# Folding the key weights in two half-height array tiles, and the last chunk's last products by column halves

## The chip, the cores and the metric

The kernel runs on one core of a Trainium2 chip. Its time is the device time of one execution, in microseconds (us). The matrix engine is called PE (its weight loads PEld), the vector engine DVE, the scalar engine ACT, GpSimd POOL, and SP is the engine whose queue issues most transfers. PE writes its results to PSUM, which is cut into banks of 128 partitions by 512 floats; ACT and DVE read them from there.

## The reference

For x of 2048 rows and 512 columns the reference returns `g * a + (1 - g) * b`, with a gate `g = sigmoid(sum(x * gate_w))` for each row.

`a` is linear attention with 32 heads of 16 columns:

```python
pk = einsum("bhsd,hdf->bhsf", k, w_phi)          # the same for q
phi_k = concatenate([softmax(pk), softmax(-pk)])
kv = einsum("bhsf,bhsd->bhfd", phi_k, v);  z = phi_k summed over s
o = (phi_q @ kv) / (phi_q @ z + 1e-6);  a = o @ wo
```

`b` is a feed-forward layer of width 1792: `relu(x @ w1 + b1) ** 2 @ w2 + b2`.

`pk` is `x @ wk` and then a 16 by 16 matrix for each head, so the two weights can be multiplied once, ahead of all rows: `x @ (wk w_phi)`. That product is the fold.

## The kernel before

**Precision.** Each float operand is split into a rounded high part and the rest (`split`, L58: ACT copies the high part, DVE subtracts it for the low part). A product is three matmuls (`mm3`, L66 to L70): high with high, high with low, low with high.

**Stages.** The feed-forward width is worked in two sweeps of 7 pieces of 128; each sweep passes over four row blocks of 512 rows. `work_list` (L510) lists these 56 steps. A step has an "up" product (`up`, 4 x 3 matmuls into bank `u`), relu and square on ACT and a split (`hidden`, L301), and two steps later a "down" product (`down`, L316) into four banks `d0` to `d3`, one for each chunk of 128 rows. The attention work is dealt between these steps: `at(slot, f)` (L464) puts a function at a half step. In the first sweep come the key fold, and for each chunk of 128 rows the key projection (`do_k`), its exponentials (`exps`, L191), the value projection (`do_v`) and the sum over rows (`do_kv`); in the second come the queries.

**The fold.** `load_fold` brings the transposed weight in four row tiles and `w_phi` as a block-diagonal matrix. `fold` (L138) makes the folded weight for one piece k of 128 rows: four float matmuls of 128 rows by 128 columns into one bank, then one split of 512 columns into `wkh`, `wkl`. `do_fold` (L323) is called for k = 0, 1 at slot 3 and for k = 2, 3 at slot 4 (L473), so that PE sees two blocks of eight matmuls, each put right after an up product. The banks come from two pools, `ps_a` and `ps_b`, in turn (`bank`, L50); after the last key fold `ps_b` is given to the sum over rows, and one bank is left for the key and value projections.

**What sets the order.** The framework orders the work of each engine by priority and by dependences that it finds; `tc.high_priority` lifts the splits, and `tc.issue_after` puts work behind a named instruction. Each engine works its own list in order. Tiles of a pool are reused in turn, so that a transfer into a buffer waits until the last reader of the buffer's previous content is done: the four `in` buffers are freed by the low-part subtractions on DVE.

**The end.** In the last step the products of the last two pieces are done chunk by chunk (L540 to L543), six matmuls of 512 columns for each. After each chunk DVE scales and adds the result (L560). For the last chunk that is done in two column halves, each with its own transfer to the output, one issued by SP and one by ACT.

A float matmul (not one of the rounded type) appears as two records in the profile: the 32 key-fold records are 16 matmuls.

Of the kernel before, what the change touches and what calls it, by code (L numbers as in the profile page):

```python
# [9 lines left out]
F32R = mybir.dt.float32r  # L10
# [6 lines left out]
P = 128  # L17
S, D, H, DH, F = 2048, 512, 32, 16, 1792
NK = D // P
SB = 512  # L20
NB = S // SB
NC = SB // P
NF = F // P
NFH = NF // 2
# [3 lines left out]
AHEAD = 150  # L28
# [3 lines left out]
def tile_gated_mix(ctx: ExitStack, tc: tile.TileContext, xT, xn, wqT, wkT, wphi, wv, wo, w1, b1, w2, b2, gw, out):  # L32
    nc = tc.nc
# [4 lines left out]
    wpool = pool("wpool", 1)  # L38
# [8 lines left out]
    banks = [ps_a, ps_b]  # L47
    taken = [0]

    def bank(name):  # L50
        p = banks[taken[0] % len(banks)]
        taken[0] += 1
        return p.tile([P, 512], F32, tag="s", name=name)
# [4 lines left out]
    def split(src, hi, lo, ehi, elo):  # L58
        if ehi is nc.scalar:
            i = nc.scalar.activation(hi, src, AF.Copy)  # L60
        else:
            i = ehi.tensor_copy(hi, src)
        elo.tensor_tensor(lo, src, hi.bitcast(F32), ALU.subtract)  # L63
        return i

    def mm3(o, a, b, sa, sb, first, last):  # L66
        (ah, al), (bh, bl) = a, b
        nc.tensor.matmul(o, ah[:, sa], bh[:, sb], start=first, stop=False)  # L68
        nc.tensor.matmul(o, ah[:, sa], bl[:, sb], start=False, stop=False)  # L69
        return nc.tensor.matmul(o, al[:, sa], bh[:, sb], start=False, stop=last)  # L70

    ALL = slice(0, 512)
    halves = (slice(0, 256), slice(256, 512))
# [7 lines left out]
    def row():  # L81
        return work.tile([P, D], F32, tag="row", name="row", bufs=6)
# [26 lines left out]
    st, up_w, down_w = {}, {}, {}  # L109
# [28 lines left out]
    def fold(loaded, nm, k):  # L138
        wph, *t = loaded
        ps = bank(f"fold{nm}{k}")  # L140
        for g in range(NK):
            nc.tensor.matmul(ps[:, g * P:(g + 1) * P], t[g][:, k * P:(k + 1) * P], wph[:, g * P:(g + 1) * P],
                             start=True, stop=True)
        hi = wpool.tile([P, 512], F32R, tag=f"wah{k}", name=f"w{nm}h{k}")
        lo = wpool.tile([P, 512], F32R, tag=f"wal{k}", name=f"w{nm}l{k}")
        with tc.high_priority(offset=AHEAD):
            split(ps, hi, lo, nc.scalar, nc.vector)
        return hi, lo

    def load_w(src, nm):  # L150
        res = []
        for k in range(NK):
            if nm == "o":

                t = stage.tile([P, 512], F32, tag="in", name="in")
                for q in range(4):
                    s = 64 * (4 * (k % 2) + q) + 32 * (k // 2)
                    nc.sync.dma_start(t[32 * q:32 * q + 32, :], src[s:s + 32, :])
            else:
                t = load(src[k * P:(k + 1) * P, :])  # L160
            hi = wpool.tile([P, 512], F32R, tag=f"wbh{k}", name=f"w{nm}h{k}")
            lo = wpool.tile([P, 512], F32R, tag=f"wbl{k}", name=f"w{nm}l{k}")
            split(t, hi, lo, nc.scalar, nc.vector)
            res.append((hi, lo))
        return res
# [18 lines left out]
    def project(c, xs, ws, nm):  # L184
        ps = bank(nm)
        sc = slice(c * P, (c + 1) * P)
        for k in range(NK):
            mm3(ps, xs[k], ws[k], sc, ALL, k == 0, k == NK - 1)
        return ps
# [99 lines left out]
    def attended(o, u, wos):  # L289
        ps = bank("att")  # L290
        for r in range(2):
            for t in range(2):
                mm3(ps, o[r], wos[2 * r + t], slice((2 * t + u) * P, (2 * t + u + 1) * P), ALL,
                    r + t == 0, r + t == 2)
        return ps


    def up_step(ps, k, xs, wf):
        st["up"] = mm3(ps, wf, xs[k], slice(k * P, (k + 1) * P), ALL, k == 0, k == NK - 1)
# [13 lines left out]
            up_step(ps, k, xs, wf)  # L313
        return hidden(fc, ps)

    def down(t, c, dps):  # L316
        sw, b, i = work_list[t]
        mm3(dps[c], hid[t], down_w[sw * NFH + i], slice(c * P, (c + 1) * P), ALL, i == 0, i == NFH - 1)

    def do_wT(wT):  # L320
        st["wT"] = load_fold(wT)
# [1 line left out]
    def do_fold(nm, k):  # L323
        with tc.issue_after(st["up"].ins):
            st["wa", nm, k] = fold(st["wT"], nm, k)
        if k == NK - 1:
            st["wa"] = [st["wa", nm, i] for i in range(NK)]
            if nm == "k":
                banks.pop()

    def do_w(src, nm):
        st["wb"] = load_w(src, nm)
# [131 lines left out]
    def at(slot, f, *a):  # L464
        steps.setdefault(int(slot), []).append(lambda: f(*a))
# [4 lines left out]
        at(2 * (fc - LAG) - 2, do_w1_first, fc)  # L470
        at(2 * (fc - LAG) - (2 if fc == LAG + 1 else 1), do_w2, fc)
    at(0, do_wT, wkT)
    for k in range(NK):  # L473
        at(3 + k // 2, do_fold, "k", k)
    at(1, do_w, wv, "v")
    for b in range(NB):
        for c in range(NC):
            s = b * SL + 3 * c - 3 if b else 7 + c
# [3 lines left out]
        for c in range(NC):  # L482
            n = b * NC + c
            s = 5 + 2.9 * n
# [5 lines left out]
    for k in range(NK):  # L490
        at(49 + k, do_fold, "q", k)
# [7 lines left out]
    for p in range(NB * NC // 2):  # L499
        n, s = 2 * p, 54 + 6 * p  # L500
# [10 lines left out]
    hid, last = {}, len(work_list) - 1  # L511

    def do_up(t):
        if t < len(work_list):
            sw, b, i = work_list[t]
            fc = sw * NFH + i
            hid[t] = up(fc, st["x", sw * NB + b], up_w[fc])
# [12 lines left out]
    dps = None  # L530
    for t, (sw, b, i) in enumerate(work_list):
        for f in steps.get(2 * t, ()):
            f()
        do_up(t + LAG)
        for f in steps.get(2 * t + 1, ()):
            f()
        if i == 0:
            dps = [ps_d.tile([P, 512], F32, tag="d", name=f"d{c}") for c in range(NC)]

        now = () if t == last - 1 else (t - 1, t) if t == last else (t,)  # L540
        for c in range(NC):
            for u in now:
                down(u, c, dps)  # L543
        if i < NFH - 1:
            continue
        for c in range(NC):
            n = b * NC + c
            done = ("f", n) in st
            if sw == 0:
                o = row()  # L550
                nc.scalar.activation(o, b2b, AF.Copy, scale=rest[:, n:n + 1])
            else:
                if not done:
                    st["f", n] = row()
                    nc.sync.dma_start(st["f", n], part[n])
                o = st["f", n]
            dst = part[n] if sw == 0 else out[n * P:(n + 1) * P, :]
            for j, s in enumerate(halves if n == NB * NC - 1 and done else (ALL,)):
                with tc.high_priority(offset=AHEAD):
                    nc.vector.scalar_tensor_tensor(o[:, s], dps[c][:, s], rest[:, n:n + 1], o[:, s], ALU.mult, ALU.add)  # L560
                if sw == 0 or done:
                    (nc.scalar if j else nc.sync).dma_start(dst[:, s], o[:, s])
# [47 lines left out]
```

## Time and profile before

| what | value |
|---|---|
| median of three timings | 533.31 us (532.88 to 533.75) |
| the profiled execution's own time | 533.63 us |
| its span, first to last instruction | 531.8 us |
| PE busy | 521.5 us, 98% |
| PEld, DVE, ACT, POOL busy | 417.5, 355.9, 234.7, 76.8 us |
| key-fold records on PE (L142) | 32, mean 281 ns |
| granted PE clock | 1.000 |

A row of the timeline has the start in us, the length in us, engine, line, operation, what is written from what, the shape, and how many instructions are merged; square brackets hold the idle time before it and what ended it. PE's matmuls overlap and their ends are modelled, so starts are what to compare: where the engine streams, the next start comes sooner than the length. A row of the waits reads: who waited for whom, total us, times, longest. Groups by line give busy us and mean ns of one, and then the idle time before them. Transfers by issue have KB and the median us from issue to landing.

### The profile page before, as it was taken

The page shows a single profiled execution, that of the slowest core. Times are in us where ns is not written, and L with a number is a line of the kernel's source. Part 1 is how long each engine was busy: PE and PEld are TensorE (multiplying, and loading weights), DVE is VectorE, ACT ScalarE, POOL GpSimd, SP SyncE. Part 2 cuts the span into 40 slices and gives each one's busy share as a digit, 9 for nine tenths or more (in the row PEclk, how much of TensorE's full clock was granted, in tenths as well). Part 3 has the DMA queues.
Part 4 walks back from the last instruction along what each step waited for, and adds up shares of the span by engine and source line. Part 5 has one row for each costly group of instructions (what it writes and reads, how often), then busy time and mean ns, then how long its engine had stood idle before and what let it go on. Part 6 is the DMA issues. An engine that isn't in the chain of part 4 may idle for free.

```text
span 531.8 us, 8944 instructions
## 1 busy us (share of the span) xinstructions
PE 521.5 (98%) x3475; PEld 417.5 (79%) x3475; DVE 355.9 (67%) x608; ACT 234.7 (44%) x404; POOL 76.8 (14%) x60
## 2 busy tenths in 40 slices
PE   8998999999999999999999999999999999999997
PEld 3886888888888887887878878787887878787775
DVE  4688536743465434567579998998878887779423
ACT  3874333622435224254654564353435353535230
POOL 2001111111110011011103121202111111112000
PEclk9999999999999999999999999999999999999999
DMA  7974004200042000415346113134102311023102
GB/s 236 297 240 138 2 0 160 76 6 1 1 159 70 10 1 21 160 41 160 88 139 222 35 41 122 53 118 137 40 22 79 119 51 30 22 70 100 49 1 79
DMA packets 30834, 45.16 MB, mean 85 GB/s; under 512 B 5704, under 2 KB 12360, under 8 KB 30792
## 3 DMA queue, kind: packets, MB, share of 16 engines
q1 hardware_dynamic: 30328, 44.20, 27.0%
q8 instruction: 27, 0.44, 0.3%
q10 hardware_dynamic: 432, 0.39, 0.2%
q14 instruction: 15, 0.12, 0.1%
q0 software_dynamic: 32, 0.01, 0.0%
HBM read 29.89 MB, written 8.39 MB: 72 GB/s over the span
## 4 chain that ended last, share of the span: by engine, by line
PE 72%; DVE 10%; DMA 6%; SPq 5%; ACT 3%; POOL 2%; issue 2%; DVEq 0%; ACTq 0%; POOLq 0%
PE u L68 7%; PE d L69 7%; PE d L70 7%; PE d L68 7%; PE u L70 7%; PE u L69 7%; SPq L257 4%; PE v L68 3%; PE k L68 3%; PE v L69 3%; PE v L70 3%; PE k L70 3%; PE k L69 3%; PE kvps L221 2%; DMA in<-in_xT 2%; PE att L68 2%
## 5 line engine op out<-in xcount | busy, mean ns | idle before, releaser
L303 ACT ACTIVATE r<-u,b1c 128x512 f32<-128x512 f32 x56 | 38.5, 687 | 151.3 <-PE u L70 148.0
L68 PE MATMUL d<-w2h,hh 128*128 128x512 f32 x224 | 87.5, 391 | 0.0
L69 PE MATMUL d<-w2l,hh 128*128 128x512 f32 x224 | 87.3, 390 | 0.0
L70 PE MATMUL d<-w2h,hl 128*128 128x512 f32 x224 | 87.1, 389 | 0.0
L68 PE MATMUL u<-xh,w1h 128*128 128x512 f32 x220 | 86.8, 395 | 0.1
L70 PE MATMUL u<-xh,w1l 128*128 128x512 f32 x220 | 85.7, 390 | 0.5 <-DVE w1l L63 0.5
L69 PE MATMUL u<-xl,w1h 128*128 128x512 f32 x220 | 85.8, 390 | 0.0
L63 DVE TENSOR_TENSOR hl<-r,hh 128x512 fp32r<-128x512 f32 x56 | 43.0, 769 | 54.8 <-ACT hh L60 54.7
L231 POOL TENSOR_TENSOR ez<-e,z 128x512 f32<-128x512 f32 x32 | 41.4, 1317 | 188.3 <-ACT e L204 188.3
L213 POOL TENSOR_TENSOR e<-e,r 128x1024 f32<-128x1024 f32 x16 | 32.3, 2017 | 205.0 <-DVE r L209 158.3
L207 DVE TENSOR_REDUCE sm<-e 128x64 f32<-128x1024 f32 x32 | 39.0, 1218 | 28.5 <-ACT e L204 28.4
L68 PEld LDWEIGHTS u<-xh,w1h 128*128 128x128 f32 x220 | 41.3, 188 | 12.0 <-issue 1.6
L70 PEld LDWEIGHTS d<-w2h,hl 128*128 128x128 f32 x224 | 42.0, 188 | 8.7
L68 PEld LDWEIGHTS d<-w2h,hh 128*128 128x128 f32 x224 | 42.0, 188 | 8.7
L69 PEld LDWEIGHTS d<-w2l,hh 128*128 128x128 f32 x224 | 42.1, 188 | 8.6
L70 PEld LDWEIGHTS u<-xh,w1l 128*128 128x128 f32 x220 | 41.3, 188 | 9.5 <-DVE w1l L63 0.9
L69 PEld LDWEIGHTS u<-xl,w1h 128*128 128x128 f32 x220 | 41.3, 188 | 8.2
L204 ACT ACTIVATE e<-e 128x1024 f32<-128x1024 f32 x32 | 33.8, 1055 | 23.7 <-DVE e L202 23.5
L255 ACT ACTIVATE phiT<-tb 32x256 f32<-32x256 f32 x64 | 26.5, 413 | 35.1 <-DVE tb L249 34.4
L60 ACT ACTIVATE hh<-r 128x512 fp32r<-128x512 f32 x56 | 35.2, 628 | 1.3
L304 ACT ACTIVATE r<-r 128x512 f32<-128x512 f32 x56 | 35.1, 627 | 1.0
L199 DVE TENSOR_REDUCE mx<-k 128x32 f32<-128x512 f32 x16 | 11.0, 688 | 26.3 <-PE k L70 26.3
(106 smaller groups left out, 888.5 us busy)
## 6 DMA issues: line engine op xcount, KB each, us to landing
in<-in_xT SPq DMA_DIRECT2D x32, 256.0 KB, 3.9
in<-in_w SPq DMA_DIRECT2D x24, 256.0 KB, 3.2
phiT<-tb SPq DMA_DIRECT2D x192, 32.0 KB, 1.8
row<-in_xn SPq DMA_DIRECT2D x16, 256.0 KB, 3.2
part<-row SPq DMA_DIRECT2D x16, 256.0 KB, 2.0
row<-part SPq DMA_DIRECT2D x16, 256.0 KB, 3.5
out<-row SPq DMA_DIRECT2D x15, 256.0 KB, 2.2
row<-in_wkT SPq DMA_DIRECT2D x4, 256.0 KB, 6.0
```

Of the source, the lines that this page charges most:

```text
L60: i = nc.scalar.activation(hi, src, AF.Copy)
L63: elo.tensor_tensor(lo, src, hi.bitcast(F32), ALU.subtract)
L68: nc.tensor.matmul(o, ah[:, sa], bh[:, sb], start=first, stop=False)
L69: nc.tensor.matmul(o, ah[:, sa], bl[:, sb], start=False, stop=False)
L70: return nc.tensor.matmul(o, al[:, sa], bh[:, sb], start=False, stop=last)
L204: nc.scalar.activation(ef, ef, AF.Exp)
L207: nc.vector.tensor_reduce(sm, e3, AX.X, ALU.add)
L213: eng.tensor_tensor(e3, e3, w.unsqueeze(2).to_broadcast([P, 2 * H, DH]), ALU.mult)
L231: nc.gpsimd.tensor_tensor(ez[:, hs, :], e3[:, hs, :], zbc[half], ALU.mult)
L255: nc.scalar.activation(dst, src, AF.Copy)
L303: nc.scalar.activation(r, ps, AF.Relu, bias=b1c[:, fc:fc + 1])
L304: nc.scalar.activation(r, r, AF.Square)
```

## The change

The query folds are left as they are. The key folds are done two pieces at a time by a new function, `fold_pair`. It takes both banks. Each 128-row matmul becomes two of 64 rows: the upper 64 rows go with the first 64 columns of the block-diagonal matrix into the first bank, the lower 64 rows with the other 64 columns into the second. Each bank so holds one half of the columns of both pieces, and each piece is split in two parts of 256 columns that lie in strips of 64 in the result. The order of matmuls is piece, row tile, half.

In the last step, for the last chunk alone, `down` is called for the first 256 columns with both pieces, and then for the other 256. `mm3` gets a flag for this, with which every product is marked as the end of its group. The evaluation in two column halves behind it is as it was.

```diff
-    def mm3(o, a, b, sa, sb, first, last):
+    def mm3(o, a, b, sa, sb, first, last, skip=False):
         (ah, al), (bh, bl) = a, b
-        nc.tensor.matmul(o, ah[:, sa], bh[:, sb], start=first, stop=False)
+        nc.tensor.matmul(o, ah[:, sa], bh[:, sb], start=first, stop=skip, skip_group_check=skip)
...
+    def fold_pair(loaded, nm, ks):
+        wph, *t = loaded
+        pss = [bank(f"fold{nm}{ks[0]}_{r}") for r in range(2)]
+        for i, k in enumerate(ks):
+            for g in range(NK):
+                for r in range(2):
+                    rows, o = slice(64 * r, 64 * r + 64), (NK * i + g) * 64
+                    nc.tensor.matmul(pss[r][:, o:o + 64], t[g][rows, k * P:(k + 1) * P],
+                                     wph[rows, g * P + 64 * r:g * P + 64 * r + 64],
+                                     start=True, stop=True, skip_group_check=True)
+        res = []
+        for i, k in enumerate(ks):
+            hi = wpool.tile([P, 512], F32R, tag=f"wah{k}", name=f"w{nm}h{k}")
+            lo = wpool.tile([P, 512], F32R, tag=f"wal{k}", name=f"w{nm}l{k}")
+            part_of = lambda w, r: w.rearrange("p (g r f) -> p g r f", g=NK, r=2)[:, :, r, :]
+            for r in range(2):
+                with tc.high_priority(offset=AHEAD):
+                    split(pss[r][:, 256 * i:256 * i + 256].rearrange("p (g f) -> p g f", f=64),
+                          part_of(hi, r), part_of(lo, r), nc.scalar, nc.vector)
+            res.append((hi, lo))
+        return res
...
-    def down(t, c, dps):
+    def down(t, c, dps, cols=ALL):
         sw, b, i = work_list[t]
-        mm3(dps[c], hid[t], down_w[sw * NFH + i], slice(c * P, (c + 1) * P), ALL, i == 0, i == NFH - 1)
+        mm3(dps[c][:, cols], hid[t], down_w[sw * NFH + i], slice(c * P, (c + 1) * P), cols, i == 0, i == NFH - 1,
+            (sw, b, c) == (1, NB - 1, NC - 1))
...
+    def do_fold_pair(nm, k):
+        with tc.issue_after(st["up"].ins):
+            st["wa", nm, k], st["wa", nm, k + 1] = fold_pair(st["wT"], nm, (k, k + 1))
+        if k == NK - 2:
+            st["wa"] = [st["wa", nm, i] for i in range(NK)]
+            banks.pop()
...
-    for k in range(NK):
-        at(3 + k // 2, do_fold, "k", k)
+    for k in range(0, NK, 2):
+        at(3 + k // 2, do_fold_pair, "k", k)
...
         for c in range(NC):
-            for u in now:
-                down(u, c, dps)
+            for s in halves if t == last and c == NC - 1 else (ALL,):
+                for u in now:
+                    down(u, c, dps, s)
```

More of the change, by code (lines that the diff above doesn't have):

```diff
@@ L64, in split @@
         return i
-    def mm3(o, a, b, sa, sb, first, last):
+    def mm3(o, a, b, sa, sb, first, last, skip=False):
         (ah, al), (bh, bl) = a, b
-        nc.tensor.matmul(o, ah[:, sa], bh[:, sb], start=first, stop=False)
-        nc.tensor.matmul(o, ah[:, sa], bl[:, sb], start=False, stop=False)
-        return nc.tensor.matmul(o, al[:, sa], bh[:, sb], start=False, stop=last)
+        nc.tensor.matmul(o, ah[:, sa], bh[:, sb], start=first, stop=skip, skip_group_check=skip)
+        nc.tensor.matmul(o, ah[:, sa], bl[:, sb], start=False, stop=skip, skip_group_check=skip)
+        return nc.tensor.matmul(o, al[:, sa], bh[:, sb], start=False, stop=last or skip, skip_group_check=skip)
     ALL = slice(0, 512)
@@ L327, in do_fold @@
             st["wa"] = [st["wa", nm, i] for i in range(NK)]
-            if nm == "k":
-                banks.pop()
+    def do_fold_pair(nm, k):
[4 more added lines that the diff above has]
+            banks.pop()
     def do_w(src, nm):
```

## The prediction

> **What bounds the kernel.** I read the page's table of engines first, then the timeline of PE for every place where one matmul starts later than its stream would let it, then the waits behind those places.
>
> ```profile
> span 531.8 us, 8944 instructions
> PE 521.5 (98%) x3475; PEld 417.5 (79%) x3475; DVE 355.9 (67%) x608; ACT 234.7 (44%) x404; POOL 76.8 (14%) x60
> ```
>
> TensorE's order of work is nearly the whole span; other engines matter where PE waits for them. The waits between 17 and 50 us, where the folds stand:
>
> ```profile
> PE k L68 <- ACT vext L407: 1.2, 1, 1.2
> ...
> PE v L68 <- DVE e L202: 0.8, 1, 0.8
> PEld foldk L142 <- DVE wkl L63: 0.8, 2, 0.5
> ```
>
> Two of them come after the folds, so this stretch has slack of its own: what PE loses at the folds can come off the two later waits. The timeline:
>
> ```profile
> 22.71 0.39 PE L70 MATMUL u<-xh,w1l 128*128 128x512 f32 x1
> 22.94 1.95 PE L142 MATMUL foldk<-row 128*128 128x128 f32 x16
> 24.64 0.48 PE L68 MATMUL d<-w2h,hh 128*128 128x512 f32 x1
> 24.95 0.40 PE L69 MATMUL d<-w2l,hh 128*128 128x512 f32 x1
> ...
> 27.23 0.39 PE L70 MATMUL d<-w2h,hl 128*128 128x512 f32 x1
> ...
> 27.74 2.35 PE L142 MATMUL foldk<-row 128*128 128x128 f32 x16
> ...
> 29.85 0.47 PE L68 MATMUL u<-xh,w1h 128*128 128x512 f32 x1
> 30.16 0.39 PE L69 MATMUL u<-xl,w1h 128*128 128x512 f32 x1
> ...
> 32.70 0.39 PE L68 MATMUL k<-wkh,xh 128*128 128x512 f32 x1
> ```
>
> ```profile
> 41.82 0.47 PE L68 MATMUL v<-wvh,xh 128*128 128x512 f32 x1 [0.81 <-DVE e L202]
> ...
> 46.94 0.50 PE L68 MATMUL k<-wkh,xh 128*128 128x512 f32 x1 [1.21 <-ACT vext L407]
> ```
>
> A 512-column product starts every 0.227 us (22.71 to 22.94). A fold block of 8 matmuls is 16 records in 1.70 us, 0.106 each; from the last u to the second d it is 2.24 us, 1.79 above two spacings. PE could have begun the second block at 27.46 but began at 27.74, waiting for the first split.
>
> **First fold block: rows halved, records doubled.** After: 32 records of 64 rows by 64 columns, 16 in each half of the array. The trace has the half-array form only in `numer`:
>
> ```profile
> 312.77 0.39 PE L70 MATMUL d<-w2h,hl 128*128 128x512 f32 x1
> 313.09 0.62 PE L268 MATMUL num<-phiT,kvb 64*32 64x256 f32 x2
> ...
> 314.12 0.21 PEld L268 LDWEIGHTS num<-phiT,kvb 64*32 64x32 f32 x16 [0.90 <-ACT r L304]
> ...
> 315.17 0.19 PEld L68 LDWEIGHTS u<-xh,w1h 128*128 128x128 f32 x1 [0.41 <-issue]
> 315.17 0.50 PE L68 MATMUL u<-xh,w1h 128*128 128x512 f32 x1
> 315.28 0.19 PEld L69 LDWEIGHTS u<-xl,w1h 128*128 128x128 f32 x1
> 315.51 0.40 PE L69 MATMUL u<-xl,w1h 128*128 128x512 f32 x1
> ```
>
> Two things are seen. Where PE goes into the tiled form a start comes 0.32 after the last one instead of 0.227, and coming out 0.34 (315.17 to 315.51): with the drain between some 0.25 us for each block, which before does not pay. And a 128-column load holds the path 0.11 us (315.17 to 315.28, nothing to hide it), which is the fold's 0.106 a record: the old fold is as much load-bound as product-bound. The new loads are still 128 columns wide. No row has a 64-row, 128-column load. Bounds: 0.055 (half), so 16 x 0.055 = 0.9 us a block; 0.11 with the two halves side by side, 1.8; 0.11 one after the other, 3.5. I take 1.8: sixteen 64-row loads begin and end within 0.21 us, so tiles do load side by side, and nothing shows that fewer rows load quicker. Block: 1.8 + 0.25 against 1.79, so +0.25, range -0.65 to +2.0.
>
> [...]
>
> **Second fold block: what it now waits for.** This is the bigger term. Before, block two's first four matmuls wait for one split and the next four for another; after, each bank holds half of both key tiles, so it needs the splits of both. In the built program of the changed kernel ACT does, after the square of r: hh, both halves of wkh0, w1h, w2h, both of wkh1; DVE does hl, both of wkl0, w1l, both of wkl1. hh and hl now stand ahead.
>
> ```profile
> 25.32 0.63 ACT L304 ACTIVATE r<-r 128x512 f32<-128x512 f32 x1
> 25.86 0.58 ACT L60 ACTIVATE wkh<-foldk 128x512 fp32r<-128x512 f32 x1
> ...
> 27.75 0.62 ACT L60 ACTIVATE hh<-r 128x512 fp32r<-128x512 f32 x1
> ```
>
> ```profile
> 27.00 0.68 DVE L63 TENSOR_TENSOR wkl<-foldk,wkh 128x512 fp32r<-128x512 f32 x1
> 27.60 0.68 DVE L63 TENSOR_TENSOR w1l<-in,w1h 128x512 fp32r<-128x512 f32 x1
> ...
> 29.40 0.68 DVE L63 TENSOR_TENSOR w2l<-in,w2h 128x512 fp32r<-128x512 f32 x1
> ```
>
> ACT takes 0.53 for a 512-wide row in a queue, DVE 0.60 (27.00 to 27.60). A half: ACT 0.41 alone, 0.30 in the queue (the page's phiT copy of 256 columns, 0.413 mean); DVE 0.41, 0.33 in the queue, from the pair of 256-wide rows in the last fence.
>
> ```profile
> L255 ACT ACTIVATE phiT<-tb 32x256 f32<-32x256 f32 x64 | 26.5, 413 | 35.1 <-DVE tb L249 34.4
> ```
>
> ACT: hh 25.98 (after the square) to 26.60, wkh0 26.50 and 26.80, w1h 27.10, w2h 27.62, wkh1 28.14 and 28.44 to 28.85. DVE: hl 27.0, wkl0 27.60 and 27.93, w1l 28.26, wkl1 28.86 to 29.27 and 29.19 to 29.60. PE reaches the block at 27.70 and starts at 29.32; the second bank may follow at 29.66, three matmuls later in PE's order. The last record starts near 31.4, u near 31.6, its second row at 31.9 against 30.16: +1.75. The key projection, 11 spacings on, starts at 34.4 against 32.70.
>
> Behind block two ACT's order is both halves of wkh2, xh1 of the next rows, wkh3's first half, xh2, wkh3's second half. xh2 waits for a transfer that landed at 34.75 before (the first of the two at 34.77):
>
> ```profile
> 28.31 2.73 SPq L78 DMA_DIRECT2D in<-in_xT  x3
> ...
> 34.77 1.32 ACT L60 ACTIVATE xh<-in 128x512 fp32r<-128x512 f32 x2 [1.32 <-DMA in<-in_xT]
> ```
>
> ```profile
> in<-in_xT SPq DMA_DIRECT2D x32, 256.0 KB, 3.9
> ```
>
> It goes out when w2l has freed its buffer, at 30.2 against 30.08 (29.40 + 0.68), so it lands at 34.87; wkh3's second half 35.4 to 35.8, wkl3's to 36.24. The projection wants them at 36.44 and 36.67: hidden by 0.4 us, thanks only to PE being late. On SP's queue the first w load after xT stands, and one xn load moves ahead of the next w load; that one waits for xl1 anyway (34.3), so nothing is added there.
>
> **What is given back.** After the keys PE does 24 products (5.4 us) and then v. PE gets there at 42.6, against 41.82, of which 0.8 us was a wait for DVE's e. DVE's part of that wait goes: a gate multiplication stands behind the exps now, so mx starts at 38.95 and e ends at 41.4.
>
> ```profile
> 39.20 0.69 DVE L199 TENSOR_REDUCE mx<-k 128x32 f32<-128x512 f32 x1
> ...
> 45.69 0.72 ACT L551 ACTIVATE row<-b2b,rest 128x512 f32<-128x512 f32 x1 [0.85 <-DVE rest L181]
> 46.31 0.58 ACT L407 ACTIVATE vext<-v 128x512 f32<-128x512 f32 x1
> ```
>
> The next wait, the second key chunk behind vext, is the one that decides. vext stands behind two bias rows on ACT, and the second waits for a rest on DVE that now has the moved multiplication in front. e's exponent 41.46 to 42.5, sm 42.55, w2l 43.7, r 44.3, the multiplication 44.9, rest 45.8; bias row 46.1, vext 46.7 to 47.3; k at 47.35 against 46.94. So +0.4 is all that is left of +1.75: this chain, not PE, sets it. From the third key chunk on both kernels issue the same work in the same order on every engine, so it stays.
>
> **The last chunk: columns in two halves.** Six products of 512 columns become twelve of 256, all with their own load.
>
> ```profile
> 526.43 0.39 PE L68 MATMUL d<-w2h,hh 128*128 128x512 f32 x1
> ...
> 527.57 0.39 PE L70 MATMUL d<-w2h,hl 128*128 128x512 f32 x1
> 527.99 0.88 DVE L560 SCALAR_TENSOR_TENSOR row<-d,rest,row 128x256 f32<-128x256 f32 x2 [0.61 <-PE d L70]
> 528.90 0.35 ACTq L562 DMA_DIRECT2D out<-row  x1
> ```
>
> If the first half's evaluation began under the second half's products, the second would start at 527.97 instead of 528.39: -0.4. But in the built program DVE's first half waits for the count that only the very last product raises, and its second half for nothing: both halves stand behind all twelve, as before. Price of the twelve: 0.11 each, load under product, as the fold's records ran with both at that length: 1.34 against 6 x 0.227 = 1.36. Bounds: -0.4 (early half) and, load and product in turn, 12 x 0.22 = 2.7, +1.3. I take 0. The tail's 3.8 us from 527.99 to the end of the span stay.
>
> **Sum.** 0.4 + 0. The profiled execution is 533.63 (span 531.8 and 1.8 around it), so 534.0; it lies 0.3 over the median 533.31, against which I forecast 533.7.
>
> **Rivals.** (1) *Slower: the x transfer in ACT's queue.* xh2 now stands ahead of wkh3's second half, and everything on DVE to vext follows it. Each us by which it lands after 34.87 reaches k whole; from 0.7 late the loss passes 0.2%. For it: two xn loads go out close behind it. Against: the median of its kind is 3.9 us, and the forecast already gives it 4.7 (30.2 to 34.87). One us: 534.7. (2) *Slower: the twelve loads are not hidden.* +1.3 on the end itself with the 0.4: 535.0. Against: the fold's 0.106. (3) *The halves load in turn.* Both blocks 1.8 longer; block two ends at 33.0, v starts at 44.1, vext at 47.2, k at 47.85: +0.9, 534.2, and with drains up to 534.5. (4) *Faster: the halves run at 0.055 and vext is not held.* v starts at 41.6 when e ends, vext at 44.5, k at 45.2: -1.7, 531.6. Against: the bias row's wait for rest. [...] (5) *The change does nothing at the end*, which is in my forecast already; were it to work, 533.3.
>
> **How the numbers follow.** Forecast 0.60 (532.5, where PE alone sets k after an unheld vext, to 534.3); (1) 0.15; (2) 0.06; (3) 0.09, of which 0.05 beyond 0.2%; (4) 0.10. 0.2%, 1.07 us, is about what a measurement here can tell from no change. Slower 0.26, same 0.64, faster 0.10. The range 532.5 to 535.0 leaves out (4) and the far part of (1).
>
> **What would show it.** Block two starts at 29.3 after 1.6 us of PE idle put down to wkl; each block lasts 1.8 to 2.1 us; k at 34.4, v at 42.6, the second k at 47.3; both 256-wide rows of the last chunk behind the last product. Blocks of 0.9 or 3.5 us, or a second k off by over a us, would prove me wrong.

## The result, and the profile after

The changed kernel takes 536.04 us (median; 533.42 to 539.16), the kernel before, run beside it, 533.65 (532.30 to 535.53). The ratio is 1.0043, with a 95% interval of 1.0028 to 1.0059: 0.4% slower, where 533.7 us was forecast and the range ended at 535.0. The profiled execution took 537.46 us, 1.4 above the median, so it shows more of the loss than a usual one: 3.9 us of span over before's 531.8.

From the page of the changed kernel, the span, TensorE's row, and the queue that brings program code:

```profile
span 535.7 us, 9033 instructions
PE 524.4 (98%) x3513; PEld 420.4 (78%) x3513; DVE 355.8 (66%) x612; ACT 235.6 (44%) x408; POOL 77.5 (14%) x60
...
q8 instruction: 28, 0.46, 0.4%
```

And that queue on the page of before:

```profile
q8 instruction: 27, 0.44, 0.3%
```

TensorE (PE) is busy 2.9 us longer with only 38 matmul records more; that is too much for light products. There are 89 instructions and one code transfer more. Both facts matter below.

First the folds, in PE's timeline of the changed kernel (start, duration, line, product; in brackets the idle time before it and what ended it):

```profile
22.86 0.39 PE L70 MATMUL u<-xh,w1l 128*128 128x512 f32 x1
23.18 2.00 PE L159 MATMUL foldk<-row 64*128 64x64 f32 x32
...
25.45 0.39 PE L69 MATMUL d<-w2l,hh 128*128 128x512 f32 x1
...
27.74 0.39 PE L70 MATMUL d<-w2h,hl 128*128 128x512 f32 x1
29.95 2.95 PE L159 MATMUL foldk<-row 64*128 64x64 f32 x32 [1.83 <-DVE wkl L63]
...
33.42 0.63 PE L69 MATMUL u<-xl,w1h 128*128 128x512 f32 x1
33.85 0.63 PE L70 MATMUL u<-xh,w1l 128*128 128x512 f32 x1
...
38.11 0.46 PE L68 MATMUL k<-wkh,xh 128*128 128x512 f32 x1
...
50.23 0.48 PE L68 MATMUL k<-wkh,xh 128*128 128x512 f32 x1
```

The wait stands where it was forecast. What follows was not forecast: behind the block a product comes every 0.427 us (33.42 to 33.85), not every 0.227. The same stretch by windows. A row has the stretch and its length, then the busy time and the number of instructions of PE, PEld, DVE, ACT and POOL; the number behind these is PEclk, the granted TensorE clock; the last two are the DMA share and GB/s:

```profile
27.90:29.90 2.00, 0.23 (x2) 0.00 (x0) 2.00 (x6) 1.81 (x4) 0.00 (x0) 1.00 0.56 205
29.90:32.80 2.90, 2.85 (x32) 2.79 (x32) 2.71 (x7) 1.11 (x4) 0.00 (x0) 0.76 0.53 167
32.80:38.20 5.40, 5.40 (x14) 4.21 (x14) 4.26 (x11) 3.40 (x9) 0.00 (x0) 0.50 0.86 265
38.20:44.00 5.80, 5.80 (x27) 4.79 (x26) 3.75 (x9) 4.35 (x9) 0.00 (x0) 1.00 0.40 130
```

The clock was at half for 2 x (2.90 x 0.24 + 5.40 x 0.50) = 6.8 us, which costs 3.4 us. Before, over the same stretch, it was 1.00:

```profile
33.00:38.20 5.20, 5.20 (x25) 4.30 (x24) 4.48 (x14) 3.83 (x8) 0.00 (x0) 1.00 0.80 266
```

The second key chunk, forecast at 47.35, starts at 50.23 (before 46.94). Some 0.3 us are given back in the waits behind it, and 3.0 us remain at the first product of the key-value sums (62.88 against 59.86).

The other part of the loss is far away, at the last pair of chunks. PE's last `num` products, which wait for phiT, and SP's queue of the 24 transfers that bring phiT, before:

```profile
503.61 0.62 PE L268 MATMUL num<-phiT,kvb 64*32 64x256 f32 x2
504.84 1.09 PE L268 MATMUL num<-phiT,kvb 64*32 64x256 f32 x30 [0.61 <-DMA phiT<-tb]
...
488.23 15.08 SPq L257 DMA_DIRECT2D phiT<-tb  x24
```

And after:

```profile
506.72 0.62 PE L292 MATMUL num<-phiT,kvb 64*32 64x256 f32 x2
508.67 1.09 PE L292 MATMUL num<-phiT,kvb 64*32 64x256 f32 x30 [1.33 <-DMA phiT<-tb]
...
491.33 15.80 SPq L281 DMA_DIRECT2D phiT<-tb  x24
```

The queue takes 0.72 us longer for the same 24 transfers, and PE waits 0.72 us longer. So 3.0 + 0.7 + 0.1 (the last chunk, below) make up 3.8 of the 3.9 us of this execution.

The granted clock over the whole span goes with the time from run to run. In the 22 runs of the changed kernel it is 0.989 to 0.999; the five at 0.999 take 533.42 to 534.12 us, the seven at 0.994 or less 537.10 to 539.16. In before's runs, where it is listed, it was 0.998 to 1.000 in all but one, which had 0.996 and took 535.77 us.

The last chunk:

```profile
530.22 0.28 PE L68 MATMUL d<-w2h,hh 128*128 128x256 f32 x1
...
531.53 0.28 PE L70 MATMUL d<-w2h,hl 128*128 128x256 f32 x1
531.85 0.88 DVE L591 SCALAR_TENSOR_TENSOR row<-d,rest,row 128x256 f32<-128x256 f32 x2 [0.68 <-PE d L70]
532.75 0.35 ACTq L593 DMA_DIRECT2D out<-row  x1
```

Twelve products take 1.43 us (11 spacings of 0.119 and one more) in place of 1.36, and VectorE's two halves both stand behind the last of them.

### The profile page after: what moved, and what is told of

Same layout as the page of the kernel before. It is cut to its first block, busy times and chain, and to the rows that moved or that the text cites. A ratio compares the mean times of both kernels' runs of the same rounds, so it can differ in the third digit from the quotient of the medians.

```text
span 535.7 us, 9033 instructions
## 1 busy us (share of the span) xinstructions
PE 524.4 (98%) x3513; PEld 420.4 (78%) x3513; DVE 355.8 (66%) x612; ACT 235.6 (44%) x408; POOL 77.5 (14%) x60
## 4 chain that ended last, share of the span: by engine, by line
PE 75%; DVE 10%; SPq 5%; DMA 3%; ACT 3%; POOL 2%; issue 2%; DVEq 0%; ACTq 0%; POOLq 0%
PE u L68 7%; PE u L70 7%; PE u L69 7%; PE d L68 7%; PE d L70 7%; PE d L69 7%; SPq L281 4%; PE v L68 3%; PE k L68 3%; PE v L69 3%; PE k L69 3%; PE k L70 3%; PE v L70 3%; PE kvps L245 2%; POOL ez L255 2%; PE att L68 2%
## 5 line engine op out<-in xcount | busy, mean ns | idle before, releaser
L68 PE MATMUL u<-xh,w1h 128*128 128x512 f32 x220 | 87.9, 399 | 0.1
L68 PE MATMUL d<-w2h,hh 128*128 128x512 f32 (+1 forms) x226 | 87.9, 389 | 0.0
L69 PE MATMUL d<-w2l,hh 128*128 128x512 f32 (+1 forms) x226 | 87.6, 388 | 0.0
L70 PE MATMUL d<-w2h,hl 128*128 128x512 f32 (+1 forms) x226 | 87.5, 387 | 0.0
L63 DVE TENSOR_TENSOR hl<-r,hh 128x512 fp32r<-128x512 f32 x56 | 41.9, 748 | 54.8 <-ACT hh L60 54.7
```

## The experiments

Four theories were set against each other. T: PE idles ahead of the second fold block, its clock then falls to half for some us, and that is the loss. R1: the longer chain from the splits to the block costs by itself. R2: the half-height products lower the clock, whatever stands ahead of them. R3: the halves at the end cost. A fifth, L, came up on the way, for the phiT wait: TensorE's program comes in blocks by queue q8 (27 transfers of 0.44 MB before, 28 of 0.46 MB after: 16 KB each), and one of these now falls among the phiT transfers. Every run was timed in five rounds beside the kernel before. "Idle" in the table is PE's idle time ahead of the second fold block, "phiT" its last wait for phiT, both in us as the timeline of the run's profile has them; "clock" is the granted clock over all its runs.

| run | us | ratio (95%) | clock | idle | phiT |
|---|---|---|---|---|---|
| before | 533.65 | 1 | 0.996 to 1.000 | under 0.2 | 0.61 |
| changed | 536.04 | 1.0043 (1.0028, 1.0059) | 0.989 to 0.999 | 1.83 | 1.33 |
| fold_only | 536.76 | 1.0049 (1.0032, 1.0065) | 0.994 to 0.997 | 2.36 | 1.17 |
| tail_only | 533.47 | 0.9994 (0.9983, 1.0005) | 0.998 to 1.000 | 0.50 | 0.61 |
| fill8 | 538.97 | 1.009 (1.007, 1.011) | 0.996 to 0.999 | 0.19 | 1.61 |
| old_wait | 533.29 | 0.9998 (0.9985, 1.0011) | 0.996 to 1.000 | 0.65 | 0.61 |
| fill_pin8 | 536.08 | 1.0041 (1.0025, 1.0058) | 0.996 to 1.000 | under 0.2 | 1.30 |
| old_long | 535.44 | 1.0026 (1.0015, 1.0038) | 0.994 to 1.000 | 2.92 | 0.62 |
| moved_pin | 536.16 | 1.0037 (1.0023, 1.0051) | 0.996 to 0.997 | under 0.2 | 1.75 |
| moved_old | 534.59 | 1.0004 (0.9992, 1.0017) | 0.998 to 1.000 | under 0.2 | 0.63 |
| before_pad | 534.52 | 1.0014 (1.0002, 1.0025) | 0.998 to 1.000 | under 0.2 | 1.31 |
| after_pad | 535.05 | 1.0031 (1.0014, 1.0049) | 0.990 to 1.000 | 1.10 | 0.63 |
| moved_pad | 532.78 | 0.9983 (0.9972, 0.9995) | 0.998 to 1.000 | under 0.2 | 0.63 |
| before_pad240 | 534.10 | 1.0006 (0.9996, 1.0016) | 0.998 to 1.000 | under 0.2 | 0.61 |

**Each part alone.** `fold_only` takes the changed kernel and gives it the undivided tail; `tail_only` takes the old folds and the divided tail.

```diff
# fold_only, against the changed kernel
-            (sw, b, c) == (1, NB - 1, NC - 1))
+            False)
...
-            for s in halves if t == last and c == NC - 1 else (ALL,):
-                for u in now:
-                    down(u, c, dps, s)
+            for u in now:
+                down(u, c, dps)
# tail_only, against the changed kernel
+            if nm == "k":
+                banks.pop()
...
-    for k in range(0, NK, 2):
-        at(3 + k // 2, do_fold_pair, "k", k)
+    for k in range(NK):
+        at(3 + k // 2, do_fold, "k", k)
```

> The folds in two array tiles as in the changed kernel, the last row chunk's products as before it. T (TensorE's clock falls to half for some 6 us after the idle 1.8 us ahead of the second fold block): clock under 1 in most runs, spread between 533.5 and 538, the median near 536.0; the second block's products go from 0.11 us a pair to 0.21 and the products behind it from 0.227 us to 0.427 us until about 38 us. If the halves of the last chunk are what costs (R3), the time is that of the kernel before, 533.7, and the granted clock 1.00.

> The folds as before, the last row chunk's last products for half of the columns, then the others. T: granted clock 1.00, 533.5 to 533.9, equal to the kernel before: the twelve products are a few hundredths longer and VectorE's first half still begins behind the last of them. R3: all of the loss is here, 536, with TensorE's last record to the end longer than before.

The folds alone carry the whole loss, with a clock of 0.994 to 0.997 and a wait of 2.36 us; the tail alone is level with before. R3 is out.

**Filling the idle time.** `fill8` has PE work through the wait with products that nobody reads.

```diff
+    def fill():
+        o = ps_u.tile([P, SB], F32, tag="u", name="fill")
+        w, x = up_w[0][0], st["x", 0][0][0]
+        for _ in range(8):
+            last_fill = nc.tensor.matmul(o, w[:, :P], x, start=True, stop=True)
+        return last_fill
...
     def do_fold_pair(nm, k):
+        if k:
+            fill()
```

> The changed kernel with eight products more, of 512 columns, into a spare bank ahead of the second fold block, whose result nobody reads: TensorE works through what was the idle 1.8 us (8 x 0.227 = 1.8). T: the clock stays at 1.00, the products behind the block stay at 0.227 us, and the time is 533.5 to 534.3. R1 (the longer chain from the first block's splits to the second block, or the light loads themselves, is what costs, and not the idling): second block at the same 29.9, time 536 as in the changed kernel. R2 (the half-height products themselves lower the clock, whatever lies ahead of them): clock still under 1, 535 to 537.

538.97 us fits none of the theories. Its PE timeline and windows:

```profile
27.91 1.98 PE L358 MATMUL fill<-xh,w1h 128*128 128x512 f32 x8
30.08 2.30 PE L159 MATMUL foldk<-row 64*128 64x64 f32 x32 [0.19 <-DVE wkl L63]
38.26 0.76 PE L68 MATMUL k<-wkh,xh 128*128 128x512 f32 x1 [2.71 <-DVE wkl L63]
...
30.00:33.00 3.00, 2.92 (x35) 2.76 (x36) 2.81 (x8) 0.55 (x2) 0.00 (x0) 1.00 0.47 156
...
38.30:41.50 3.20, 3.20 (x8) 2.52 (x9) 3.18 (x8) 3.20 (x8) 0.00 (x0) 0.52 0.78 277
```

The block without a wait keeps the clock at 1.00 (30 to 33 us), so R2 in its plain form is out: in this execution the half-height products alone didn't lower it. But the planner, which saw PE later, put two x splits ahead of the second pair's key splits on ScalarE, and these wait for x transfers (1.26 and 2.56 us there). PE then idled 2.71 us ahead of the key projection, and there the clock fell: T's mechanism, in another place. That is close to my rival (1), produced by the repair.

`fill_pin8` therefore holds the x splits behind the key splits, and fills with eight products by a tile of noughts.

```diff
+                with tc.issue_after(st["ws", 2, k // 2, k % 2].ins):   # block one's x, k = 1 to 3
+                    split(t, hi, lo, nc.scalar, nc.vector)
...
+        if t == 1:
+            for _ in range(8):
+                nc.tensor.matmul(dps[3], nought, st["x", 0][0][0], start=False, stop=False)
```

> The changed kernel with eight products by a tile of noughts more, added into the last chunk's sum behind the last product ahead of the second fold block (they change no value), and with block one's x splits held behind the key weights' splits on ScalarE, so that the projection doesn't wait for x transfers as it did in the first filled kernel. T: TensorE idles less than 0.5 us ahead of the block, the clock is at 1.00 from 28 to 44 us, the products behind it come every 0.227 us, and the time is 533.4 to 534.4 with a clock of 0.999 or more. R1 (the longer chain from split to second block costs by itself): the second block still begins near 29.9 and the time is 535.5 to 536.5 at a clock of 1.00. R2 (the half-height products lower the clock): clock under 0.998 and 535 to 537.

In the profiled execution (0.999, 535.98 us) the clock from 28 to 44 us is 1.00, as T has it; but three of the eight runs have a clock of 0.996 or 0.997, where T had 0.999 or more, and the time is 536.08, as R1 has it. It doesn't decide: the filler itself takes 2.0 us of PE's time, at the last `num` products the profiled execution is 1.6 us behind before (505.23 against 503.61), and the phiT wait of 1.30 us adds 0.7. This run showed that something besides the clock at the folds was lost. R1 is answered better by the changed kernel's own runs: the program, and so the chain, is the same in all 22, and the five at a clock of 0.999 take 533.42 to 534.12 us, about what before takes. None of the five was profiled, so that their wait was as long is not shown.

**The wait with the old folds.** `old_wait` swaps the two banks for the second pair, so that the block waits for the second split.

```diff
+        if (nm, k) == ("k", 2):
+            taken[0] += 1
         ps = bank(f"fold{nm}{k}")
```

> The kernel before, with the two banks of the fold swapped for the second pair, so that it waits for the second split of the first pair and not for the first: TensorE idles about 1.2 us longer (VectorE's two splits end 27.7 and 28.9), 1.6 us in all, with folds of the full height and an unchanged order on every engine. T: idling is enough, the clock falls to half behind the block as in the changed kernel, at least in some runs: clock 0.993 to 0.998 and 535 to 537. R2 (only the half-height form lowers the clock): clock 1.00 and 533.5 to 534.2, since the 1.2 us are taken up by the waits behind it as in my sum.

The wait came out at 0.65 us and not 1.6, since PE itself reached the block later; the median is that of before. Four of its eleven runs have a clock of 0.998 or less and take 534.4 to 535.7 us, the others 532.5 to 533.3. Inconclusive at this dose. `old_long` makes the key splits in halves besides, and holds the products behind the block behind it.

```diff
-            split(ps, hi, lo, nc.scalar, nc.vector)
+            for s in halves if nm == "k" else (ALL,):
+                st["ws"] = split(ps[:, s], hi[:, s], lo[:, s], nc.scalar, nc.vector)
...
+            with tc.issue_after(st["folded"].ins):   # "folded": the fold's last matmul
+                do_up(t + LAG)
```

> The kernel before with folds of the full height, its two banks swapped for the second pair, its key splits made in halves as in the changed kernel and the products behind the second block held behind it, so that TensorE has nothing to do until the last half split of the first pair: it should idle 1.3 to 1.9 us ahead of the block. T (idling is what lowers the clock): clock at half for some us in the stretch from 30 to 38 us in most runs, clock 0.994 to 0.998, 534.5 to 536.5. R2 (only the half-height products behind an idle stretch do it): clock at 1.00 and 533.5 to 534.5.

```profile
30.29 3.75 PE L148 MATMUL foldk<-row 128*128 128x128 f32 x16 [2.92 <-DVE wkl L63]
...
27.40:30.30 2.90, 0.01 (x1) 0.04 (x1) 2.90 (x7) 2.85 (x7) 0.00 (x0) 0.85 0.54 195
30.30:34.00 3.70, 3.70 (x17) 3.70 (x18) 2.89 (x8) 0.90 (x2) 0.00 (x0) 0.50 0.87 244
34.00:36.20 2.20, 2.20 (x7) 1.72 (x6) 1.43 (x4) 1.91 (x6) 0.00 (x0) 0.50 0.94 243
```

Folds of the full height, an idle 2.9 us, and the clock falls to half before the block even begins, for 2 x (0.44 + 1.85 + 1.10) = 6.8 us. So idling is enough, at this length: the wait is 2.92 us where 1.3 to 1.9 was expected, and longer than the 1.83 of the changed kernel. 535.44 us, with no longer phiT wait.

**Moving the block behind other work.** `moved_pin` puts twelve up products between the first pair's splits and the second block; `moved_old` does so with the old folds (and leaves the loads and splits of x where they were).

```diff
# moved_pin, against the changed kernel (with the x splits held as in fill_pin8)
-        at(3 + k // 2, do_fold_pair, "k", k)
+        at(3 + k, do_fold_pair, "k", k)
-            at(s, do_k, b, c)
+            at(s if n else 6, do_k, b, c)
-        at(b * SL + 4, do_x, b + 1)
+        at(b * SL + (4 if b else 5), do_x, b + 1)
```

> The changed kernel with the second fold block two slots later, so that twelve products of the up projection stand between the first block's splits and it, with the key projection behind the next twelve down products. T: no idle stretch ahead of the block, clock 0.999 or more, 533.0 to 534.3, at least 1.7 us under the changed kernel. R2: the clock falls all the same, 535 to 537.

> The same shift with the folds of the kernel before and its undivided tail: a version that might beat both, if the two short waits ahead of its fold blocks are worth anything. T: 533.0 to 533.8 at a clock of 0.999 or more, the same as the kernel before within 0.2%, as its waits there (0.8 us in two) are taken up by those behind them.

`moved_old` is level with before by the ratio, as expected (534.59 us, 533.0 to 533.8 forecast; the kernel before beside it took 534.11). `moved_pin` was expected at 533.0 to 534.3 and took 536.16. There is no wait at the second block, and the key-value sums begin at 59.6 us, where before's begin at 59.86. All of the loss is at the last pair:

```profile
505.90 1.09 PE L296 MATMUL num<-phiT,kvb 64*32 64x256 f32 x30 [1.75 <-DMA phiT<-tb]
...
505.50:507.30 1.80, 1.40 (x32) 0.90 (x33) 0.00 (x0) 0.24 (x1) 0.00 (x0) 1.00 0.00 0
507.30:510.70 3.40, 3.40 (x10) 2.63 (x9) 1.29 (x2) 0.84 (x2) 0.00 (x0) 0.51 0.00 0
```

A longer wait for phiT, and behind it 3.4 us at half clock once more. The five kernels with the old folds so far show a phiT queue of 15.08 or 15.09 us and a wait of 0.61 to 0.63 at this point; the five with the new folds 15.64 to 16.21 and 1.17 to 1.75. The transfers are the same, in the same order. SP's queue and the DMA queues in the stretch where the time is lost, in the changed kernel (500.9 to 502.5) and in before (498 to 500):

```profile
500.76 1.94 SPq L281 DMA_DIRECT2D phiT<-tb  x2
...
q8 instruction: 1, 0.02, 3.8%
```

```profile
497.65 2.49 SPq L257 DMA_DIRECT2D phiT<-tb  x4
```

Before, four issues take 2.49 us, 0.63 from one to the next; after, two take 1.94, and within them the code queue q8 moves one block of 16 KB. The chain of the critical path (start, length, what) has the issue that was held, 1.31 us where the others take 0.59:

```profile
501.39 1.31 SPq L281
```

The trace's transfer records have 27 such blocks in before and 28 after. From the first of them to the last it is one per 254 weight loads and matmuls in before (6600 from 23.41 to 505.89 us, 26 spacings) and one per 252 after (6810 from 23.14 to 525.62 us, 27 spacings). In the changed kernel TensorE's program is longer (7026 loads and matmuls against 6950), so the blocks fall elsewhere: one at 501.4 us, at the 17th of the 24 phiT issues. In before the blocks nearest to the last phiT sequence came at 484.4 and 505.9, 3.9 us ahead of its start and 2.6 us behind its end. This is L. (An expectation below puts the changed kernel's block at 501.0; by the DMA view it is the one at 501.4.)

**Moving the blocks.** Eleven opening products by noughts, which stand there while the first data is on its way, are made into many small ones. That shifts all of TensorE's later code; the order of work on the other engines is the same in the traces.

```diff
-        idle(11)
+        for _ in range(46):                       # before_pad; 78 in after_pad and moved_pad
+            nc.tensor.matmul(st["warm"][:32, :64], st["zeros"][:, :32], st["zeros"][:, :64], start=True, stop=True)
+        idle(5)                                   # 1 in after_pad and moved_pad
# before_pad240: 127 products of 16 columns, idle(4)
```

> The kernel before with its eleven opening products of 512 noughts made into 46 of 64 columns and 5 of 512: the same time on TensorE, some 80 TensorE instructions more, the order of every other engine unchanged. L (TensorE's program comes in blocks of 16 KB, one per 256 instructions; a block that comes while SP issues the 24 phiT transfers of the last pair holds one issue up): the block that came at 505.9 comes near 499, one phiT issue takes 1.1 to 1.7 us in place of 0.59, TensorE waits 1.0 to 1.8 us for phiT in place of 0.6, and the time is 534.3 to 536, with the clock under 1 where the wait is long enough. Without L: 533.7 and a wait of 0.6.

> The changed kernel with its opening products made into 78 small ones and one of 512, some 136 TensorE instructions more, the order of all engines otherwise unchanged, so that the block that came at 501.0 comes near 489.5, ahead of the last pair's phiT issues. L: wait for phiT back at 0.6 us, and the time 0.7 us or more under the changed kernel, 534.8 to 535.6; the wait ahead of the second fold block and the half clock behind it remain (T). Without L: 536.0.

> The kernel with the second fold block two slots later, with the same opening as the last one. T and L together: neither an idle stretch of over a microsecond ahead of the fold block nor a long wait for phiT, clock 0.999 or more, 532.8 to 533.8, that is 2.4 us or more under moved_pin and at the kernel before's time. T alone (no L): 536 as moved_pin was.

> The kernel before with its opening in 127 products of 16 columns and 4 of 512: some 240 TensorE instructions more than before, nearly a whole 16 KB block (256), so that the blocks come almost where they came in the kernel before, one near 486, ahead of the last pair's phiT issues. L (where the block falls counts, not how many instructions there are): wait for phiT back at 0.6 us and a time within 0.5 us of the kernel before, 533.0 to 534.0, although it has three times as many more instructions as the kernel whose wait was 1.3 us. If more instructions, or the small opening products, cost by themselves: 1 us or more above the kernel before, 534.5 or higher.

The last `num` products of `before_pad`, `after_pad`, `moved_pad` and `before_pad240`, in this order, with the phiT queue of each:

```profile
504.92 1.09 PE L268 MATMUL num<-phiT,kvb 64*32 64x256 f32 x30 [1.31 <-DMA phiT<-tb]
487.61 15.77 SPq L257 DMA_DIRECT2D phiT<-tb  x24
```

```profile
505.63 1.09 PE L292 MATMUL num<-phiT,kvb 64*32 64x256 f32 x30 [0.63 <-DMA phiT<-tb]
489.01 15.09 SPq L281 DMA_DIRECT2D phiT<-tb  x24
```

```profile
503.99 1.09 PE L296 MATMUL num<-phiT,kvb 64*32 64x256 f32 x30 [0.63 <-DMA phiT<-tb]
487.37 15.09 SPq L285 DMA_DIRECT2D phiT<-tb  x24
```

```profile
505.94 1.09 PE L268 MATMUL num<-phiT,kvb 64*32 64x256 f32 x30 [0.61 <-DMA phiT<-tb]
489.33 15.08 SPq L257 DMA_DIRECT2D phiT<-tb  x24
```

L holds from both sides for the wait. The kernel before gets it, and 0.14% (0.02 to 0.25), once a block is moved among its phiT transfers; three times as many added instructions, which move a block past them, bring the wait back to 0.61. In time the second half is weaker: `before_pad240` took 534.10 us where 533.0 to 534.0 was expected (before beside it 533.42), and its interval holds 1 but also overlaps that of `before_pad`. The changed kernel loses the wait at the last pair: its ratio goes from 1.0043 to 1.0031. The two intervals overlap; by the ratios L was about a quarter of the loss, an estimate.

But the padding moved a code block into the first pair's phiT transfers as well, in `after_pad` and in `moved_pad`: at 299.0 and 296.8 us, where it holds one issue for 1.08 and 1.02 us, and the first wait for phiT is 0.94 and 0.87 us in place of before's 0.45. Before, and then in `after_pad` with the issue that was held:

```profile
314.15 1.09 PE L268 MATMUL num<-phiT,kvb 64*32 64x256 f32 x30 [0.45 <-DMA phiT<-tb]
```

```profile
299.17 1.08 SPq L281
314.94 1.09 PE L292 MATMUL num<-phiT,kvb 64*32 64x256 f32 x30 [0.94 <-DMA phiT<-tb]
```

So L is not wholly gone in these two; that it shows where the block falls, a third time, speaks for it. T is still in `after_pad`: its block waits 1.10 us, 3.4 us at half clock follow, and its runs spread as the changed kernel's do. In the profiled execution, one of the shorter (534.42 us), the slack takes up nearly all of that: the key-value sums begin at 60.01, 0.15 behind before.

`moved_pad`, without the wait at the block and without the long one at the last pair, takes 532.78 us, 0.9983 of before (0.9972 to 0.9995), and beats both kernels. `before_pad240` speaks against the small opening products as what gains it. How its 0.17% divides between the half-height folds, the moved block, the held x splits and the padding was not tried; moving the old folds gained nothing (1.0004).

## Why the prediction was wrong

**First fold block: right.** Predicted +0.25 us; from the last u to the second d it is 2.59 us in place of 2.24, +0.35. The new block's 32 records last 2.00 us and the old block's 16 lasted 1.95, so a pair of half-height loads takes no less than one load of 128 rows, as the sum had it; the two halves load side by side (the first pair begins and ends within 0.19 us, row in the last section). The rivals (3) and (4) are out.

**Second fold block: the wait right, what it does wrong.** Predicted: start at 29.32 after 1.6 us of idle time. Measured: 29.95 after 1.83, put down to wkl as predicted. Of the 0.63 us, 0.5 are hl on DVE, which starts at 27.52 and not at 27.0: DVE's gate product ahead of it waited for a transfer of x rows. (The sum's 0.33 us for half a row in DVE's queue is not in the rows that it names, where two take 0.88; the key splits show it, 0.74 for two, so that reading was luck.) The step that failed is the next one: "The last record starts near 31.4, u near 31.6 ... The key projection, 11 spacings on, starts at 34.4". It runs the fold's tail and twelve products at 0.227 us, as if a wait cost only its own length. They ran at 0.427, from about 31.4 us on, and the keys came at 38.11. What the windows of the changed kernel, `old_long` and `moved_pin` show in its place: behind a wait of 1.8 to 2.9 us the TensorE clock went to half, in the changed kernel for 6.8 us at a price of 3.4 us. A term of 1.75 us, which the slack behind it nearly swallowed, became one of over 5, which it could not.

**What is given back: right as far as it went.** Both later waits of PE vanished, and with them all the slack. "+0.4 is all that is left" was worked out for +1.75 at the keys, which no profiled run shows by itself (in `fill_pin8`, at full clock, +2.75 at the keys left +0.98 at the second key chunk); 3.0 us were left of 5.4, and the second key chunk came 2.9 us after its forecast, which the prediction itself had named as a sign of being wrong. The five runs at a clock of 0.999, 533.42 to 534.12 us, lie around the forecast, though they should carry the phiT wait too, since the program is the same, and so don't measure the +0.4.

**"From the third key chunk on both kernels issue the same work in the same order on every engine, so it stays": wrong.** The order is the same and the timing is not. 0.7 us were lost 450 us later because TensorE's longer program moved a code block among the phiT transfers. The sum put TensorE's added instructions at nothing.

**The last chunk: right.** Priced at 0, with both halves behind the last product; measured +0.07, no gain, and `tail_only` level with before.

**The rivals.** The one that decided is not among them. Rival (1), the x transfer ahead of the key splits, didn't occur in the changed kernel, but something like it did in `fill8`, for 2.7 us.

**What stays open.** How much idle time it takes. The clock fell behind 1.10 us in `after_pad` (rows in the last section) and not behind 1.74 in `moved_old`, and the changed kernel's own runs range from next to no drop to more than the 6.8 us of its profile. `moved_old`'s timeline and window:

```profile
44.61 0.47 PE L68 MATMUL v<-wvh,xh 128*128 128x512 f32 x1 [1.74 <-DVE ge L178]
...
44.70:48.00 3.30, 3.30 (x15) 2.71 (x16) 2.62 (x7) 2.86 (x5) 0.46 (x1) 1.00 0.42 157
```

In the changed kernel the drop came 1.5 us into the light fold block. That block alone never caused one in a profiled execution; whether it helps the idle time to do so was not separated, and it may. Only in `old_long` and `fill8` did the clock fall within the wait, 2.0 and 2.4 us into it; in the changed kernel, `moved_pin` and `after_pad` it fell 3.2 to 3.3 us after the wait's start, and light products filled most of the rest. In the changed kernel the clock was at 0.50 from 31.42 to 38.25 us, 6.83 us; half of that is 3.41. In the 3.41 us ahead of the drop PE was busy for 0.97 us in `fill8`, 1.37 in `old_long`, 1.58 in the changed kernel, 1.66 in `moved_pin`, and 2.32 in `after_pad`, where all but 0.2 was the fold. In `moved_old` it was busy for 1.67 us of the 3.41 up to the end of its wait, with products of 512 columns. Why the clock falls behind one such stretch and not behind another, and why runs of the same kernel differ, no run separates.

The wait itself differs too: the same fold code waited 1.83, 2.36 and 1.10 us in the changed kernel, `fold_only` and `after_pad`.

## What to carry to other kernels

A wait of one to three us on the engine that bounds the kernel is not priced at its length (here 1.83 us of waiting had 6.8 us at half clock behind it): look what the granted clock does behind it, and price the stretch behind it at half speed as a rival. Where a change adds instructions to a long stream, look where the code transfers fall: a chain of short DMA issues that the bound engine waits for can be hit or spared by a shift of a hundred instructions (here the wait for phiT was 0.61 us in before and 1.31 in `before_pad`), which makes such a difference no verdict on the change itself. And a repair that moves one engine's time can make the planner reorder another; compare the order of all engines before a run is read.

## What the runs showed of the hardware

- The half clock came in stretches of one length or twice that: 6.8 us in the changed kernel and in `old_long`, 3.4 in `moved_pin`, and in `after_pad`, 2 x (2.30 x 0.06 + 3.60 x 0.44) = 3.4, from these rows:

```profile
28.70:31.00 2.30, 2.30 (x33) 2.19 (x33) 1.72 (x4) 1.58 (x4) 0.00 (x0) 0.94 0.64 179
31.00:34.60 3.60, 3.60 (x11) 2.83 (x11) 3.15 (x10) 2.86 (x8) 0.00 (x0) 0.56 0.83 224
```

  The clock fell behind waits of 1.10 us (`after_pad`), 1.83 (the changed kernel) and 1.75 (`moved_pin`) with light products behind them, and 2.0 us into the wait of `old_long`: PE was not idle throughout the 3.41 us ahead of a drop, but busy for 0.97 to 2.32 us of them in the five profiles above (`fill8` the least, `after_pad` the most).
- A code block of 16 KB that arrived while SP issued transfers held one issue for 0.7 us longer in the changed kernel and 1.1 in `moved_pin` (15.80 and 16.21 us for the 24, against 15.08). No wait of TensorE is put down to code; the transfers of another queue were held.
- 64-row, 128-column loads of the two halves of the array ran side by side, and a pair took as long as a 128-row load: 32 fold records in 2.00 us against 16 in 1.95. The first pair of loads in the changed kernel:

```profile
23.18 0.19 PEld L159 LDWEIGHTS foldk<-row 64*128 64x128 f32 x2 [0.35 <-issue]
```
